# First input chunks loaded in three pieces of rows instead of one, two small copies issued from another queue, two matmuls moved later: a fused Fourier mixing and SoLU kernel

## The chip, the cores and the metric

The kernel runs on one core of one Trainium2 chip. The metric is device microseconds of one execution, the median over several runs. The profile is of one further execution, taken by the hardware profiler; its times are in microseconds (us) from the start of its span. PE is the matmul engine and PEld its weight load, DVE the vector engine, ACT the scalar engine, POOL GpSimd, SP the engine that here only issues DMAs; SPq and POOLq are the sequencers that issue them. L142 is line 142 of the kernel before; from L143 to the function `mean_out` the changed kernel's lines stand one higher.

## The reference

```python
# x (8, 3136, 256); w_in (256, 1024); w_out (1024, 256); g_ln (1024)
X = np.fft.fft(np.fft.fft(x, axis=1), axis=2).real      # over the sequence and over the features
t = X.reshape(25088, 256)
h = t @ w_in
sm = softmax(h)                                          # over the 1024 columns
solu = h * sm
ln = (solu - mean(solu)) / sqrt(var(solu) + 1e-6) * g_ln
out = ln @ w_out
```

All data are float32 in the device's memory, the weights in 64-bit pieces that the kernel narrows itself.

## The kernel before, in words

**The transform.** The 3136 positions are taken as 49 times 64, and the transform over the sequence is done in two matmul steps. Because only the real part is wanted, a row is always used together with its mirrored row, and the features are folded likewise before the product with `w_in`. The 8 batches go in 4 *pairs*; two batches of 49 rows are the 98 rows (`PR`) of a pair. A pair's 98 rows times 64 columns n2 are loaded in 8 *chunks* (`NC`) of 4 columns: `load` brings `xa`, the rows as they lie (L142, issued by SP, one DMA for a chunk), and `xb`, the mirrored rows (L144, an indirect DMA issued by POOL). For the first pair `rows` is 128 and not 98: 30 rows more are loaded than are used. A row of a chunk is 1024 floats, 4 KB. Chunks 0, 1, 6 and 7 lie in buffers of the pool `x`, chunks 2 to 5 in buffers named `room` that later hold `uT`.

For each chunk DVE adds the mirrored rows (`add_mirror`, L167 and L169) and folds the features (L174, L175, L182); PE makes `transform1` (L242); ACT copies the result `z` out of PSUM (L245). For the first pair this is the start of the program, and the next work on it follows from these chunks alone. SP keeps `z` in device memory (`zd`, L250), `turn` brings it back in another layout as `g` (L257, one half of the first part issued by SP and one by POOL), and `transform2` (L269) is made for each unit.

**The units.** After the start the program is a loop over 98 *units* of rows. For a unit: `transform2`, a copy to `q` (L275), a small copy `r` (`spread`, L280, SP), the product with `w_in` (`up`, L305), `even` (L318, DVE, output `ev`), `join` (L334 and L338, DVE, outputs `h` and its negated maximum `nmax`), the exponential (L346, ACT, reads `h` and `nmax`, output `u`), `product` (L353, DVE), `square` (L360, ACT), a transpose on DVE (L425, output `v`), 16 DMAs on SP for every second unit that move blocks of `v` to `uT` (L462), sums of blocks on POOL (L495, output `S`), seven block products in place of eight on PE (L502, `Ws` and `Wo` are made of `w_out`), with a copy on ACT between them (`seed`, L528), then the outputs `ot` and their stores (L600 on SP, L589 on POOL). PE's instructions of neighbouring units are interleaved.

**The half rows.** Two of the units, 90 and 91 in the order, come from rows that two batches share. One row of them (`q_half`) is computed for all batches at once by the class `Half`, in steps at units 86 to 89, and then `give` copies it into row 0 and every 32nd row of the unit's own `h` (4 rows of 4 KB) and `nmax` (4 values). These two copies are made once for each of the two units, on POOL's queue, after POOL's sums and before the run of 16 `uT` moves that SP issues at the even unit. ACT's second exponential of the unit reads them. (Such a unit runs its signs in the order 1, 0 at `join` and 0, 1 at the exponential.)

**The second weight at the start.** `raw_out`, the pieces of `w_out`, is loaded after the chunks; DVE narrows it in four steps to `Wo` (the last instruction of a step is L677). The mean of `w_out` over its rows is taken out of it: PE multiplies `ones` with the first four of the eight blocks of `Wo` (`mean_out(0)`, L782), and later with the sum of the other four, which POOL makes in `fold_out`; then `keep_mean` and `centre`.

**What sets the order.** The program is written inside `tc.manual_schedule()`: each engine runs its instructions in the order in which the code names them, and waits at each for the semaphores that the framework derives from the data. DMAs of SP count on eight semaphores in turn (`DMAHW0` to `DMAHW7` in the rows below), and each waits for the one issued eight places earlier to have landed.

Of the kernel before, what the change touches and what calls it, by code (L numbers as in the profile page):

```python
# [17 lines left out]
P = 128  # L18
# [5 lines left out]
NH = N2 // 2  # L24
PR = 2 * N1
# [30 lines left out]
def kernel(  # L56
# [76 lines left out]
    def load(pr, c, room=None):  # L133

        r = slice(pr.p * PR, (pr.p + 1) * PR)
        rows = PR if pr.p else P
        if room is None:
            xa = xpool.tile([P, CH, D], FP32, tag="xa", name="xa")
            xb = xpool.tile([P, CH, D], FP32, tag="xb", name="xb")
        else:  # L140
            xa, xb = (t.rearrange("p (l d) -> p l d", d=D) for t in room)
        nc.sync.dma_start(out=xa[0:rows], in_=x_pn[r.start : r.start + rows, c * CH + 1 : (c + 1) * CH + 1, :])  # L142
        i = pr.p * NC + c  # L143
        nc.gpsimd.indirect_dma_start(  # L144
            out=xb[0:rows].rearrange("p l d -> p (l d)"), out_offset=None, in_=x_g,
            in_offset=bass.IndirectOffsetOnAxis(ap=idx[0:rows, i : i + 1], axis=0))
        xa, xb = xa[0:PR], xb[0:PR]
        if c == NC - 1 and pr.p:
            load_zero(pr)
        pr.raw[c] = (xa, xb)  # L150
# [529 lines left out]
    class Weights:  # L680
# [91 lines left out]
            n = KF // 4 * D  # L772
            nc.gpsimd.tensor_tensor(out=self.part, in0=w[:, 0:n], in1=w[:, n:], op=ALU.add)

        def mean_out(self, half):
            if half == 0:
                self.cs = result(3)[:, 0:D]
                parts = [Wo[:, c, :] for c in range(KF // 2)]
            else:
                parts = [self.part[:, c * D : (c + 1) * D] for c in range(KF // 4)]  # L780
            for c, i in enumerate(parts):
                nc.tensor.matmul(self.cs, ones, i, start=half == 0 and c == 0, stop=half == 1 and c == KF // 4 - 1,  # L782
                                 skip_group_check=True)

        def keep_mean(self):
# [56 lines left out]
    class Half:  # L842
# [32 lines left out]

        def give(self, t):
            of = slice(4 * t.m, 4 * t.m + 4)
            nc.gpsimd.dma_start(out=t.h[1][0 : P : NH], in_=self.h[of])
            nc.gpsimd.dma_start(out=t.nmax[0 : P : NH, 1:2], in_=self.row[of, 1:2])

    with tc.manual_schedule():
        pairs = [Pair(p) for p in range(NP)]
# [124 lines left out]
        def begin(i):  # L1007

            cur = units[i]
            enter(i)  # L1010
            ps = up(cur, 0)
            if i in (2, 3):
                cur.odd = up(cur, 1)
                column(cur)
            even(cur, ps)
            if i not in (2, 3):
                cur.odd = up(cur, 1)
            second_transform(i + 2)
# [8 lines left out]
        for i in range(whole + 1):  # L1027
            cur = units[i]
            prv = units[i - 1] if i else None
            if prv:  # L1030
                turn_whole(prv, i == 1)
                if i == 1:
                    square(prv, 1)
            if i == 1:
                weights.mean_out(1)
            for s in cur.signs:
                join(cur, s)
            if i == 0:
                weights.narrow_out(3, (2,))
                weights.fold_out()  # L1040
            if 1 < i < whole:
                for o, ps in prv.wait:
                    nc.vector.tensor_copy(out=o, in_=ps)
            for s in cur.signs:
                expo(cur, s)
            if i == 1:
                weights.keep_mean()
            if i in (1, whole):
                for o, ps in prv.wait:
                    nc.scalar.copy(o, ps)  # L1050
            if i == 0:
                begin(1)
            done = units[0 if i == 2 else i - 1 : i] if i > 1 else []
            for t in done:
                stats(t)
            if i == whole:
                nxt = units[i + 1]
                enter(i + 1)
                even(nxt, up(nxt, 0))
            if i == whole:  # L1060
                other_pairs(i, ahead, "fold")
            for s in cur.signs:
                product(cur, s)
                if i < whole and s == 0:
                    square(cur, s)
            if i == 1:
                weights.centre(cur)
            if i == 2:
                weight_sums(cur)
            if i < whole:  # L1070

                if i:
                    begin(i + 1)
                if i:
                    square(cur, 1)
            else:
                for s in cur.signs:
                    square(cur, s)
                other_pairs(i, ahead, "mirror", cur)
                sums(units[1], None, part=slice(2, 4))  # L1080
                turn_both(cur)
                stats(cur)
            for work in ("mirror", "fold", "load") if i < whole else ("load",):
                other_pairs(i, ahead, work, cur)
            if i == whole - 1:
                sums(units[1], None, part=slice(0, 2))
            for t in done:
                power(t)
# [211 lines left out]
```

## Time and profile before

| | before |
|---|---|
| median of 3 runs (lowest to highest) | 1114.31 us (1113.95 to 1114.52) |
| the profiled execution's own time | 1113.99 us |
| its span, and PE's granted clock in it | 1112.2 us, 0.998 |
| PE busy | 1094.5 us, 98% |
| DVE busy | 971.2 us, 87% |
| ACT busy | 801.3 us, 72% |
| POOL busy | 786.6 us, 71% |
| DMA packets, bytes | 447594, 185.69 MB |

The time of the execution is 1.8 us over the span: what lies around the first and last instruction. An engine's share of the whole span says little of its share at the two places that the change touches, the first 90 us and the stretch of 1000 to 1025 us; those are read from windows of their own.

### The profile page before, as it was taken

The numbers are of one execution on the slowest core, as the hardware profiler recorded it, in microseconds if no ns is written. First come the engines' busy times: TensorE is split into PE (matmuls) and PEld (weight loads), VectorE is DVE, ScalarE is ACT, GpSimd is POOL, SyncE is SP. The second block draws the span as 40 slices with busy tenths as digits, with TensorE's granted clock in tenths as the row PEclk, the third lists the DMA queues.
The fourth block names the chain that finished last, engine by engine and source line by source line (L and its number), as shares of the span: only waits on it lengthen the run. The fifth ranks groups of instructions, "written<-read, shape, count | busy, mean of one in ns | idle before, by whom it ended". The sixth has DMA issues, their size and how long they took to land. (4 is left out here: it accounts for less than half of the span.)

```text
span 1112.2 us, 21997 instructions
## 1 busy us (share of the span) xinstructions
PE 1094.5 (98%) x7083; PEld 876.8 (79%) x7083; DVE 971.2 (87%) x1439; ACT 801.3 (72%) x1964; POOL 786.6 (71%) x661
## 2 busy tenths in 40 slices
PE   8899999999999999999999999999999999999998
PEld 5557878787887878788788787878878877777888
DVE  7998888889898898989989898888898898897984
ACT  5697777777777777777777777777777777676772
POOL 4066888775888878767778887856766766667665
PEclk9999999999999999999999999999999999999999
DMA  9654899878989989868989999976977878766775
GB/s 330 223 178 97 182 183 202 182 141 164 189 148 198 190 188 197 169 130 151 193 154 199 185 190 201 178 142 118 184 143 136 150 142 152 131 122 112 144 134 127
DMA packets 447594, 185.69 MB, mean 167 GB/s; under 512 B 415102, under 2 KB 429454, under 8 KB 447480
## 3 DMA queue, kind: packets, MB, share of 16 engines
q1 hardware_dynamic: 434760, 144.58, 68.5%
q0 software_dynamic: 12720, 39.69, 12.1%
q8 instruction: 58, 0.95, 0.3%
q14 instruction: 56, 0.46, 0.1%
HBM read 46.75 MB, written 38.80 MB: 77 GB/s over the span
## 5 line engine op out<-in xcount | busy, mean ns | idle before, releaser
L305 PE MATMUL ps_h<-Wi,q 128*128 128x512 f32 x768 | 346.7, 593 | 2.0 <-DVE nmax L338 1.7
L495 POOL TENSOR_TENSOR S<-uT 128x512 f32<-128x512 f32 x188 | 239.7, 1275 | 116.4 <-DVE u L353 50.6
L502 PE MATMUL ps_m<-Ws,S 128*128 128x128 f32 x2328 | 301.0, 275 | 2.5 <-POOL S L495 2.5
L502 PEld LDWEIGHTS ps_m<-Ws,S 128*128 128x128 f32 x2328 | 283.3, 192 | 7.8 <-POOL S L495 4.5
L360 ACT ACTIVATE h<-u,usum 128x1024 f32<-128x1024 f32 x196 | 225.0, 1148 | 68.6 <-DVE u L353 68.6
L305 PEld LDWEIGHTS ps_h<-Wi,q 128*128 128x128 f32 x768 | 138.4, 190 | 141.6 <-issue 136.6
L353 DVE SCALAR_TENSOR_TENSOR u<-h,u 128x1024 f32<-128x1024 f32 x196 | 233.7, 1228 | 15.9 <-ACT u L346 15.8
L346 ACT ACTIVATE u<-h,nmax 128x1024 f32<-128x1024 f32 x196 | 223.5, 1142 | 8.1 <-DMA nmax<-half 3.7
L425 DVE STREAM_TRANSPOSE v<-u 128x2048 f32<-128x2048 f32 x92 | 212.6, 2311 | 3.2
L502 PE MATMUL ps_m<-Wo,uT 128*128 128x128 f32 x1552 | 205.5, 275 | 0.0
L502 PEld LDWEIGHTS ps_m<-Wo,uT 128*128 128x128 f32 x1552 | 189.7, 192 | 2.0 <-issue 1.9
L338 DVE CUSTOM_DVE_ANT_0 h<-ev,ps_h 128x1024 f32<-128x1024 f32 x98 | 119.7, 1221 | 17.1 <-DVE ev L318 7.9
L338 DVE CUSTOM_DVE_ANT_0 h<-h,ps_h 128x1024 f32<-128x1024 f32 x96 | 117.2, 1221 | 14.0 <-ACT h L360 0.4
L589 POOL DMA_INDIRECT out_dram<-ot,idx x98 | 108.8, 1110 | 26.9 <-issue 11.5
L495 POOL TENSOR_TENSOR S<-S,uT 128x512 f32<-128x512 f32 x94 | 119.7, 1274 | 7.4
L495 POOL TENSOR_TENSOR S<-uT,S 128x512 f32<-128x512 f32 x94 | 119.8, 1275 | 7.3
L318 DVE SCALAR_TENSOR_TENSOR ev<-w_mid,r,ps_h 128x1024 f32<-128x1024 f32 x97 | 120.3, 1240 | 0.1
L502 PE MATMUL ps_m<-Ws,uT 128*128 128x128 f32 x776 | 102.7, 275 | 0.0
L502 PE MATMUL ps_m<-Wo,S 128*128 128x128 f32 x776 | 102.5, 275 | 0.0
L167 POOL TENSOR_TENSOR xa<-xa,xb 98x510 f32<-98x510 f32 (+1 forms) x48 | 59.3, 1236 | 56.8 <-DVE u L353 45.8
L537 ACT ACTIVATE ot<-ps_m,rs 128x256 f32<-128x256 f32 x97 | 45.9, 473 | 69.5 <-PE ps_m L502 50.3
L502 PEld LDWEIGHTS ps_m<-Ws,uT 128*128 128x128 f32 x776 | 94.7, 192 | 0.0
(141 smaller groups left out, 1191.7 us busy)
## 6 DMA issues: line engine op xcount, KB each, us to landing
uT<-v SPq DMA_DIRECT2D x736, 128.0 KB
out_dram<-ot SPq DMA_DIRECT2D x184, 64.0 KB
g<-zd POOLq DMA_DIRECT2D x18, 640.0 KB, 7.5
zd<-z SPq DMA_DIRECT2D x24, 400.0 KB
xa<-in_x_dram SPq DMA_DIRECT2D x24, 392.0 KB
raw_in<-in_moe_w_in_dram SPq DMA_DIRECT2D x4, 512.0 KB
xa<-in_x_dram SPq DMA_DIRECT2D x4, 512.0 KB
room<-in_x_dram SPq DMA_DIRECT2D x4, 512.0 KB
```

The lines of the kernel that those rows point to most:

```text
L167: i = engine.tensor_tensor(out=a[:, :, 1:D], in0=a[:, :, 1:D], in1=rb[:, :, D - 1 : 0 : -1], op=ALU.add)
L305: nc.tensor.matmul(ps[:, fs], t.q[:, c * P : (c + 1) * P], Wi[:, c, fs], start=True, stop=not whole_even)
L318: nc.vector.scalar_tensor_tensor(out=t.ev, in0=w_mid, scalar=t.r, in1=ps, op0=ALU.mult, op1=ALU.add)
L338: nc.vector.tensor_tensor_reduce(out=t.h[s], in0=t.h[0] if s else t.ev, in1=t.odd, scale=1.0 if s else -0.5, scalar=3.0e38, op0=ALU.add, o ...
L346: nc.scalar.activation(out=t.u[s], in_=t.h[s], func=ACT.Exp, bias=t.nmax[:, s : s + 1], scale=sign_of(t, s), accum_out=t.esum[:, s : s + 1])
L353: t.last = nc.vector.scalar_tensor_tensor(out=t.u[s], in0=t.h[s], scalar=sign_of(t, s), in1=t.u[s], op0=ALU.mult, op1=ALU.mult, accum_out= ...
L360: nc.scalar.activation(out=t.h[s], in_=t.u[s], func=ACT.Square, bias=t.usum[:, s : s + 1], scale=-float(FF), accum_out=t.ssq[:, s : s + 1])
L425: nc.vector.transpose(out=v, in_=u)
L495: i = engine.tensor_tensor(out=S[j], in0=a, in1=b, op=op)
L502: nc.tensor.matmul(o, a[:, c], b[:, c], start=start and c == 0, stop=c == n - 1, skip_group_check=True)
L537: nc.scalar.mul(out=self.t.ot[1], in_=self.PP, mul=self.rs[1])
L589: dma = nc.gpsimd.indirect_dma_start(out=out, out_offset=bass.IndirectOffsetOnAxis(ap=idx[:, i : i + 1], axis=0), in_=t.ot[s], in_offset=None)
```

## The change

It has three parts. (1) For the first pair, `xa` of a chunk is loaded in three DMAs, of rows 0 to 63, 64 to 95 and 96 to 97, instead of one of 128 rows. (2) The two copies of `give` are issued by SP instead of POOL. (3) `mean_out` is divided in three: the products of `ones` with blocks 0 and 1 of `Wo` stay where they were, those with blocks 2 and 3 come after `begin(1)` at unit 0, the last part stays.

```diff
 def load(pr, c, room=None):
...
-        nc.sync.dma_start(out=xa[0:rows], in_=x_pn[r.start : r.start + rows, c * CH + 1 : (c + 1) * CH + 1, :])
+        for a, b in ((0, PR),) if pr.p else ((0, 64), (64, 96), (96, PR)):
+            nc.sync.dma_start(out=xa[a:b], in_=x_pn[r.start + a : r.start + b, c * CH + 1 : (c + 1) * CH + 1, :])
...
-        def mean_out(self, half):
-            if half == 0:
+        def mean_out(self, part):
+            n = KF // 4
+            if part == 0:
                 self.cs = result(3)[:, 0:D]
-                parts = [Wo[:, c, :] for c in range(KF // 2)]
-            else:
-                parts = [self.part[:, c * D : (c + 1) * D] for c in range(KF // 4)]
-            for c, i in enumerate(parts):
-                nc.tensor.matmul(self.cs, ones, i, start=half == 0 and c == 0, stop=half == 1 and c == KF // 4 - 1,
+            for c in range(n):
+                i = self.part[:, c * D : (c + 1) * D] if part == 2 else Wo[:, part * n + c, :]
+                nc.tensor.matmul(self.cs, ones, i, start=part == 0 and c == 0, stop=part == 2 and c == n - 1,
                                  skip_group_check=True)
...
         def give(self, t):
             of = slice(4 * t.m, 4 * t.m + 4)
-            nc.gpsimd.dma_start(out=t.h[1][0 : P : NH], in_=self.h[of])
-            nc.gpsimd.dma_start(out=t.nmax[0 : P : NH, 1:2], in_=self.row[of, 1:2])
+            nc.sync.dma_start(out=t.h[1][0 : P : NH], in_=self.h[of])
+            nc.sync.dma_start(out=t.nmax[0 : P : NH, 1:2], in_=self.row[of, 1:2])
...
             if i == 1:
-                weights.mean_out(1)
+                weights.mean_out(2)
...
             if i == 0:
                 begin(1)
+                weights.mean_out(1)
```

What stands on SP's queue at the start, before. A row is a line, what it issues (output, input, shape), and the semaphores it waits for; `xa` and `room` are the chunks' buffers:

```order
L711 DMA gain<-in_moe_g_ln_dram 8x128
L142 DMA xa<-in_x_dram 128x1024 [waits DMAHW0_49]
L142 DMA xa<-in_x_dram 128x1024 [waits DMAHW1_49]
L142 DMA room<-in_x_dram 128x1024 [waits DMAHW2_49]
L142 DMA room<-in_x_dram 128x1024 [waits DMAHW3_49]
```

And with the change:

```order
L143 DMA xa<-in_x_dram 64x1024 [waits DMAHW0_49]
L143 DMA xa<-in_x_dram 32x1024 [waits DMAHW1_49]
L143 DMA xa<-in_x_dram 2x1024 [waits DMAHW2_49]
L143 DMA xa<-in_x_dram 64x1024 [waits DMAHW3_49]
L143 DMA xa<-in_x_dram 32x1024 [waits DMAHW4_49]
L143 DMA xa<-in_x_dram 2x1024 [waits DMAHW5_49]
L143 DMA room<-in_x_dram 64x1024 [waits DMAHW6_49]
```

Three issues stand for each one, 24 for 8 in all, and the eighth DMA ahead is two and two thirds chunks ahead instead of eight.

On SP's queue after the second of the two units with half rows, before: the stores of a unit before it, the small copy `r` of two units, and the next run of `uT` moves.

```order
L600 DMA out_dram<-ot_8896 32x2x256 [waits DMAHW5_49]
L600 DMA out_dram<-ot_8896 32x2x256 [waits DMAHW6_49]
L280 DMA r<-q 128x1x1 [waits DMAHW7_49,Activation_49]
L280 DMA r<-q 128x1x1 [waits DMAHW0_49,Activation_49]
L462 DMA uT<-v_8961 32x16x64 [waits DVE_49,DMAHW1_49,PE_49,Pool_49]
```

The same place with the change:

```order
L601 DMA out_dram<-ot_8912 32x2x256 [waits DMAHW7_49]
L601 DMA out_dram<-ot_8912 32x2x256 [waits DMAHW0_49]
L281 DMA r<-q 128x1x1 [waits DMAHW1_49,Activation_49]
L878 DMA h<-half 4x1024 [waits DMAHW2_49,DVE_49]
L879 DMA nmax<-half 4x1 [waits DMAHW3_49,DVE_49]
L281 DMA r<-q 128x1x1 [waits DMAHW4_49,Activation_49]
L463 DMA uT<-v_8977 32x16x64 [waits DVE_49,DMAHW5_49,PE_49,Pool_49]
```

The two copies stand behind the stores and the first `r`. On POOL's queue they stood, for that unit, between its sums and its store:

```order
L495 TENSOR_TENSOR S_106<-uT 128x512 [waits PE_49]
L878 DMA h<-half 4x1024 [waits DVE_49]
L879 DMA nmax<-half 4x1 [waits DVE_49]
L589 DMA out_dram<-ot_8976,idx 25088x256 [waits DMASW1_49]
L495 TENSOR_TENSOR S_105<-uT 128x512 [waits DMAHW4_49,DMAHW5_49,DMAHW3_49,DMAHW6_49,DVE_49,PE_49]
```

For the first of the two units they now stand on SP behind that unit's `r` and right ahead of the run of 16 `uT` moves.

On PE before, from the last product for the first weight on (`ps_m_104` takes the mean, `g` is the transformed half of the first pair):

```order
L731 MATMUL wps<-w_in,w_mid 128x512 x4
L782 MATMUL ps_m_104<-Wo,ones_ident 128x256 x4
L269 MATMUL ps_m_101<-T_88,g 128x128 x2
L269 MATMUL ps_m_102<-T_88,g 128x128 x2
L305 MATMUL ps_h_429<-Wi,q 128x512 x2
```

and with the change, the same place, up to the first transposes of unit 0, where the moved products now stand:

```order
L782 MATMUL ps_m_104<-Wo,ones_ident 128x256 x2
L270 MATMUL ps_m_101<-T_88,g 128x128 x2
L270 MATMUL ps_m_102<-T_88,g 128x128 x2
L306 MATMUL ps_h_443<-Wi,q 128x512 x2
L306 MATMUL ps_h_448<-Wi,q 128x512 x2
L270 MATMUL ps_m_101<-T_88,g 128x128 x2
L306 MATMUL ps_h_467<-Wi,q 128x512 x2
L306 MATMUL ps_h_472<-Wi,q 128x512 x2
L270 MATMUL ps_m_101<-T_88,g 128x128 x2
L782 MATMUL ps_m_104<-Wo,ones_ident 128x256 x2
L444 MATMUL ps_m_102<-ones_ident,u 128x128 x4
```

Two of the four products of the ones have left the place ahead of `transform2` of the first units.

## The prediction

> **What bounds the kernel now.** I read the page first. Its first two lines give PE's busy time and its share in 40 slices:
>
> ```profile
> PE 1094.5 (98%) x7083; PEld 876.8 (79%) x7083; DVE 971.2 (87%) x1439; ACT 801.3 (72%) x1964; POOL 786.6 (71%) x661
> PE   8899999999999999999999999999999999999998
> ```
>
> PE sets the time over most of the span, and is short of work at the start. Next come the stretches as windows; the columns are the window and its length, the busy time of PE, PEld, DVE, ACT and POOL, the granted clock, the DMA share and GB/s:
>
> ```profile
> 16.00:38.00 22.00, 19.68 (x81) 13.35 (x81) 18.98 (x38) 9.82 (x19) 2.84 (x3) 1.00 1.03 396
> 38.00:88.00 50.00, 45.67 (x191) 26.42 (x190) 47.33 (x85) 41.81 (x83) 22.53 (x21) 1.00 0.47 144
> 100.00:200.00 100.00, 100.00 (x656) 81.17 (x655) 89.71 (x138) 75.39 (x190) 82.50 (x66) 1.00 0.87 181
> 1000.00:1050.00 50.00, 47.52 (x310) 37.63 (x310) 42.36 (x62) 35.43 (x88) 33.94 (x31) 1.00 0.66 119
> ```
>
> From 100 us on PE has no idle time, except for 2.48 us of the window from 1000 us, where the copies of `give` are. So whatever the start loses, and whatever PE loses later, goes through to the end. In 16 to 38 us the DMA engines are full (share 1.03), and DVE then works nearly without a gap up to 88 us (47.33 of 50). So a delay of DVE at the chunks should also pass to the end. All three parts touch places where slack is small; 0.2% of the time, about what a measurement of this kernel can tell from no change, is 2.2 us.
>
> **Part 1, the chunks in pieces.** DVE's timeline has the three mirror adds of the first pair that wait for a load:
>
> ```profile
> 16.71 1.22 DVE L167 TENSOR_TENSOR xa<-xa,xb 98x1020 f32<-98x1020 f32 x1 [0.95 <-DMA xa<-in_x_dram]
> 24.39 1.22 DVE L167 TENSOR_TENSOR room<-room 98x1020 f32<-98x1020 f32 x1 [1.25 <-DMA room<-in_x_dram]
> 33.60 1.22 DVE L167 TENSOR_TENSOR xa<-xa,xb 98x1020 f32<-98x1020 f32 x1 [0.68 <-DMA xa<-in_x_dram]
> 36.20 0.68 DVE L167 TENSOR_TENSOR xa<-xa,xb 98x510 f32<-98x510 f32 x1
> ```
>
> They are chunks 0, 3 and 6; the last row is chunk 7's, with no wait. The DMA view of 16 to 24 us says how the two queues share:
>
> ```profile
> 16.00:24.00 8.00, 8.00 (x31) 5.18 (x31) 6.39 (x11) 2.88 (x7) 2.40 (x2) 1.00 1.03 409
> q0 software_dynamic: 449, 1.64, 51.5%
> q1 hardware_dynamic: 448, 1.63, 51.1%
> ```
>
> POOL's queue (`xb`, q0) and SP's (`xa`, q1) move the same, together 409 GB/s. A chunk is 128 rows of 4 KB twice, 1.05 MB, so a pair of loads takes 2.56 us; chunk 3's add at 24.39 less chunk 0's at 16.71 is 7.68, three times 2.56. The change takes 30 rows off `xa`: 401 KB and 524 KB, 2.26 us at the same rate. Counted in bytes alone a chunk would be 0.30 us shorter; but `xb` is not cut and gets half the engines, and it lands hardly before `xa` now:
>
> ```profile
> L144 POOL DMA_INDIRECT room<-in_x_dram,idx x2: 941/1014/1087, 11.2 to 12.6; - x2
> DMA to landing us min/median/max: 12.9/13.6/14.2
> ```
>
> The first of these two, chunk 3's, landed at 11.2 + 12.9 = 24.1, 0.3 us before its add. By bytes alone the gain is then that 0.3 or a little less, and chunk 6's wait of 0.68: together about 0.9 us.
>
> Against it stands what loads into fewer partitions moved. Two windows hold one alone, each on SP's queue: first the rest of the table `T`, issued at 54.20 into 64 partitions a DMA, then the second pair's `xa`, into 98:
>
> ```profile
> 54.20 1.22 SPq L716 DMA_DIRECT2D T<-in_t_tab_dram  x2
> ...
> 57.20:58.20 1.00, 0.24 (x2) 0.17 (x2) 1.00 (x3) 0.56 (x2) 1.00 (x1) 1.00 0.92 225
> 69.00:70.50 1.50, 1.20 (x4) 0.55 (x4) 1.50 (x5) 1.50 (x3) 0.86 (x1) 1.00 0.78 216
> ```
>
> With the engines 0.92 busy, 64 partitions took 225 GB/s, against 409 at 1.03 for 128. The new pieces are of 64 and 32 rows. No row shows a 32-row load from outside alone. Its ends are 112 GB/s, half of 225 by its partitions, and 409; I take 225, the row nearest in kind. Then a chunk is 96 rows of 4 KB, 393 KB at 225 GB/s = 1.75 us, and the last 2 rows with `xb`, 532 KB at 409 = 1.30 us: 3.05 instead of 2.56, 0.49 us more. Chunk 6 is the seventh pair to land, so its add starts 7 times 0.49 = 3.4 us later, and DVE's following work with it. (Chunk 7 lands 3.9 later, and had 1.1 us in hand before its add at 36.20, by the pace from chunk 6.) The ends: -0.9 us if bytes alone count; and if a piece slows all that is in flight with it, 925 KB at 225 / 0.92 = 245 GB/s is 3.78 us, 1.22 more, times seven +8.5 us. I take +3.4, since `xb` and the pieces are in flight together in every engine, and an engine that waits on a piece holds up the `xb` rows behind it only in part. The 16 more issues on SP lie ahead of the landings and cost nothing: one is 0.36 us by the row below, three a chunk are 1.1 of its 2.56 us or more, and the queue's depth of eight DMAs, two and two thirds chunks or 6.8 us, covers them. If that cover were short, the chunks would land later still.
>
> ```profile
> 22.89 0.36 SPq L142 DMA_DIRECT2D xa<-in_x_dram  x1
> ```
>
> The Trainium skill, in "SBUF — State Buffer", section "Door 1: The DMA port swizzle", says that partitions 0 to 63 reach 8 of 16 ports, and 0 to 31 the same 8, so that 32 rows move as fast as 64, at most 218 GB/s. The 225 beside it agrees for 64; by it the two pieces would take 393 KB / 218 = 1.80 us, and the part +3.8 us, where 112 GB/s for the 32 rows would give 1.17 + 1.17 us and +7.5.
>
> **Part 2, the copies of `give`.** Rows of SP, DVE, POOL, ACT and PE around the two units:
>
> ```profile
> 1001.29 13.35 SPq L462 DMA_DIRECT2D uT<-v  x16
> 1001.77 0.15 DVE L322 TENSOR_SCALAR nmax<-nmax 128x1 f32<-128x1 f32 x1
> 1002.80 0.59 POOL L879 DMA_DIRECT2D nmax<-half  x1
> 1006.71 1.15 ACT L346 ACTIVATE u<-h,nmax 128x1024 f32<-128x1024 f32 x1 [2.37 <-DMA nmax<-half]
> 1011.02 1.13 PE L502 MATMUL ps_m<-Ws,S 128*128 128x128 f32 x8 [1.46 <-POOL S L495]
> 1014.75 2.67 SPq L600 DMA_DIRECT2D out_dram<-ot  x4
> 1015.14 0.56 POOL L879 DMA_DIRECT2D nmax<-half  x1
> 1017.52 0.54 SPq L280 DMA_DIRECT2D r<-q  x1
> 1018.10 1.15 ACT L346 ACTIVATE u<-h,nmax 128x1024 f32<-128x1024 f32 x1 [1.37 <-DMA nmax<-half]
> 1022.41 1.13 PE L502 MATMUL ps_m<-Ws,S 128*128 128x128 f32 x8 [1.02 <-POOL S L495]
> ```
>
> ACT waits 2.37 and 1.37 us for the copies, and PE then 1.46 and 1.02 us. PE's releaser is named as POOL's sum, but ACT's copy `seed`, which stands behind the late exponentials on ACT, ends just before:
>
> ```profile
> 1010.65 0.27 ACT L528 COPY ps_m<-ps_m 128x128 f32<-128x128 f32 x1
> 1022.04 0.27 ACT L528 COPY ps_m<-ps_m 128x128 f32<-128x128 f32 x1
> ```
>
> The first copies, on SP, wait for DVE's `nmax` of 1001.77 only. Two issues of 0.6 us go ahead of the `uT` run. SP's small transfers at the start show the landing: `zd` is written at 41.33 and read back by the next issue at 43.27, so 1.94 us at most:
>
> ```profile
> 41.33 0.27 SPq L250 DMA_DIRECT2D zd<-z_g  x1
> 43.27 0.38 SPq L257 DMA_DIRECT2D g<-zd  x1
> ```
>
> They land at about 1001.9 + 1.2 + 1.4 = 1004.5 (POOL's landed just before 1006.71), and ACT's wait, which began at 1004.34, is gone, PE's 1.46 with it. But 0.6 us at the least and 1.2 at the most goes to the `uT` run behind them, on which everything on SP then stands. The second copies stand behind that run, the four stores and the first `r`: 1017.52 + 0.54 is 1018.06, and with 1.2 later 1019.3. Two issues of 0.6 and a landing of 0.9 to 1.9: 1021.4, for an exponential that now starts at 1018.10. So it is 3.3 us late (2.4 to 4.0) in the trace's own time; PE gets there 1.46 us earlier and then idles 1.02 + 3.3 + 1.46 = 5.8 us. As the time at which PE goes on is set by SP's queue, the first wait's gain is lost in it, and the part's sum is +3.3 us. The `uT` moves behind the copies are wanted by POOL's sums four units later, which covers 1.2 us. On POOL the two issues leave, 1.2 us a unit, where it is 34 of 50 us busy: no gain. The ends: -2.5 us if both of PE's waits go (1.46 and 1.02), +4.0.
>
> **Part 3, the products of the ones.** PE's rows, with DVE's and ACT's that decide:
>
> ```profile
> 46.19 1.13 PE L782 MATMUL ps_m<-Wo,ones_ident 128*128 128x256 f32 x4 [1.20 <-DVE Wo L677]
> 47.15 1.05 PE L269 MATMUL ps_m<-T,g 128*128 128x128 f32 x8
> 50.15 0.75 DVE L671 SCALAR_TENSOR_TENSOR S<-raw_out,top_bit,S 128x512 int32<-128x512 int32 x1
> 50.81 1.28 DVE L318 SCALAR_TENSOR_TENSOR ev<-w_mid,r,ps_h 128x1024 f32<-128x1024 f32 x1
> 58.03 2.13 PE L443 MATMUL ps_m<-ones_ident,u 128*128 128x128 f32 x13 [0.76 <-DVE u L353]
> 59.16 0.62 ACT L448 COPY uT<-ps_m 128x512 f32<-128x512 f32 x1
> ```
>
> PE waited 1.20 us for `Wo` and then took 1.0 us before `transform2`, which can now be up to 2 us earlier. But the next consumer on DVE, `ev`, begins at 50.81 straight behind DVE's own step of 50.15, with no idle time, so it gains nothing; at most about 1 us, were DVE ordered otherwise. The moved products fall in PE's idle 0.76 us ahead of 58.03 and overrun it by some 0.3, which ACT's copy at 59.16 may feel. I take 0, between -1.1 and +0.3.
>
> **The sum.** +3.4 + 3.3 + 0 = +6.7 us against the profiled execution, 1113.99 (1112.2 of span and 1.8 around it), which lies 0.3 under the median of 1114.31. On the median: 1121.0 us.
>
> **The rivals.** (a) Bytes alone count, and `give` is late: -0.9 + 3.3, 1116.7 us. For it speaks that `xb` fills the engines while a piece waits, so that the 409 GB/s may hold; against it that 225 was moved with engines 0.92 busy, not idle. The Trainium skill's page "DMA: Bandwidth & Descriptors" says in "Rules for kernel authors" that two transfers to disjoint halves share the same 16 engines and serialize, and advises one of 128 partitions; by it alone the pieces would be worth their bytes.
>
> (b) Faster: the copies on SP land in time. The place is ACT's exponential of unit 91: if SP gets to the second copies by 1016.5, that is if the `uT` run takes 3 us less than its 13.35 with no POOL issues beside it, both of PE's waits go, and with bytes alone the sum is -0.9 - 2.5: 1110.9 us. Against it: 0.83 us for each of 16 issues is the trace's own row.
>
> (c) The pieces slow the start and `give` gains: 3.4 - 2.5, 1115.2 us.
>
> (d) The pieces slow `xb` too: 8.5 + 3.3, 1126.1 us. For it: all engines serve both queues in turn.
>
> **How the numbers follow.** The two questions are nearly independent. I give contention of 3.4 with a late second copy 0.50, (a) 0.22, (b) 0.09, (c) 0.08, (d) 0.11. Faster by over 0.2% is (b), 0.09. Within 0.2%, 1112.1 to 1116.5, is (c) and somewhat under half of (a): 0.18. Slower is the rest, 0.73. The range leaves out (b) and the upper half of (d), 0.15, and takes in (c): 1115.0 to 1125.5. The likeliest case's own range is 1118.5 to 1123.5.
>
> **What would show it.** Part 1: the DMA rate in 16 to 24 us falls under 380 GB/s, and the mirror adds of chunks 3 and 6 come at about 25.9 and 37.0; a rate of 400 with chunk 3 by 24.3 shows (a). Part 2: ACT's wait for the first copy is gone, the second is issued by SP at about 1019 (plus the start's shift) and ACT and PE wait for it some 5 us. Part 3: `ev` starts no earlier against DVE's step before it. I would be wrong if the pieces, being packets of 4 KB as before, are limited only where they are alone, or if SP's `uT` run gets shorter.

## The result, and the profile after

| | before | with the change |
|---|---|---|
| median | 1114.13 us of 4 runs (1112.51 to 1114.52) | 1129.38 us of 4 runs (1127.50 to 1134.69) |
| ratio, 95% interval | | 1.0147 (1.0116 to 1.0177) |
| profiled execution: time, span, granted clock | 1113.99, 1112.2, 0.998 | 1127.50, 1125.6, 0.992 |

The change makes the kernel 15.3 us slower by the medians. The side was the forecast one; the size is over twice the 6.7 us that were forecast, and outside the range. The profiled execution is the fastest of the four and carries 13.4 us of it in its span; the traces can speak of those only.

Windows of the changed kernel, with the columns as in the prediction:

```profile
16.00:24.00 8.00, 7.27 (x25) 4.02 (x24) 5.04 (x9) 1.46 (x6) 2.25 (x3) 0.95 1.04 288
100.00:200.00 100.00, 100.00 (x644) 80.78 (x643) 86.16 (x131) 73.40 (x184) 79.95 (x65) 1.00 0.87 182
1000.00:1050.00 50.00, 43.45 (x283) 35.46 (x282) 38.55 (x58) 31.36 (x77) 27.30 (x23) 0.93 0.62 112
```

In 16 to 24 us the DMA engines are as full as before (1.04) and move 288 GB/s instead of 409. The steady part is as full as before. From 1000 us PE now lacks 6.6 us of 50, before it lacked 2.5, and the granted clock is 0.93 there.

The 13.4 us can be laid out in time with one instruction that every unit has, DVE's product. Its rows for unit 0, for a unit shortly before the half rows and for one behind them, with the change:

```profile
63.69 1.33 DVE L354 SCALAR_TENSOR_TENSOR u<-h,u 128x1024 f32<-128x1024 f32 x1
...
992.18 1.23 DVE L354 SCALAR_TENSOR_TENSOR u<-h,u 128x1024 f32<-128x1024 f32 x1 [0.16 <-ACT u L347]
...
1060.74 1.27 DVE L354 SCALAR_TENSOR_TENSOR u<-h,u 128x1024 f32<-128x1024 f32 x1 [0.30 <-ACT u L347]
```

The same instructions before:

```profile
56.63 1.33 DVE L353 SCALAR_TENSOR_TENSOR u<-h,u 128x1024 f32<-128x1024 f32 x1
...
984.00 1.23 DVE L353 SCALAR_TENSOR_TENSOR u<-h,u 128x1024 f32<-128x1024 f32 x1 [0.16 <-ACT u L346]
...
1047.31 1.28 DVE L353 SCALAR_TENSOR_TENSOR u<-h,u 128x1024 f32<-128x1024 f32 x1 [0.30 <-ACT u L346]
```

They come 7.06, 8.18 and 13.43 us later with the change. So 7.0 us are lost at the start, 5.25 at the half rows, and 1.2 in between, in two small steps (0.35 near unit 25, 0.8 near unit 50).

The start is seen in DVE's mirror adds of the changed kernel, chunks 0, 3 and 6:

```profile
18.84 1.22 DVE L168 TENSOR_TENSOR xa<-xa,xb 98x1020 f32<-98x1020 f32 x1 [2.58 <-DMA xb<-in_x_dram,idx]
28.79 1.22 DVE L168 TENSOR_TENSOR room<-room 98x1020 f32<-98x1020 f32 x1 [2.23 <-DMA room<-in_x_dram,idx]
40.19 1.22 DVE L168 TENSOR_TENSOR xa<-xa,xb 98x1020 f32<-98x1020 f32 x1 [1.71 <-DMA xa<-in_x_dram]
```

They stood at 16.71, 24.39 and 33.60: a chunk takes 3.32 us from 0 to 3 where it took 2.56. Chunk 0 is 2.1 us late already, chunk 6 is 6.6 us late. What DVE waits for at chunks 0 and 3 is now `xb`, the load that was not changed. POOL's queue (q0) in the DMA view of 16 to 24 us shows why:

```profile
q0 software_dynamic: 419, 1.54, 68.1%
q1 hardware_dynamic: 240, 0.76, 35.8%
```

The last number is the time that the packets took, as a share of 16 engines times 8 us: for q0 0.681 x 128 us / 419 = 208 ns a packet, and before 0.515 x 128 / 449 = 147 ns. These means have packets of 4 bytes in them, 42 and 48 of q0's. The trace's packets of 4 KB alone took 163 ns on both queues before; with the change they took 230 ns on `xb`'s queue and 243 ns on the pieces'. So the packets of `xb` take 1.4 times as long, with their rows and bytes unchanged, nearly as long as the pieces' own.

The half rows, rows of SP, ACT and PE:

```profile
1010.62 0.56 SPq L879 DMA_DIRECT2D nmax<-half  x1
1011.29 13.14 SPq L463 DMA_DIRECT2D uT<-v  x16
1024.54 2.36 SPq L601 DMA_DIRECT2D out_dram<-ot  x4
1027.00 0.55 SPq L281 DMA_DIRECT2D r<-q  x1
1028.37 0.54 SPq L879 DMA_DIRECT2D nmax<-half  x1
...
1012.42 1.13 ACT L347 ACTIVATE u<-h,nmax 128x1024 f32<-128x1024 f32 x1
1030.11 1.15 ACT L347 ACTIVATE u<-h,nmax 128x1024 f32<-128x1024 f32 x1 [7.67 <-DMA nmax<-half]
...
1034.41 2.05 PE L503 MATMUL ps_m<-Ws,S 128*128 128x128 f32 x8 [6.54 <-POOL S L496]
1036.25 1.61 PE L503 MATMUL ps_m<-Wo,uT 128*128 128x128 f32 x8
```

The first copies cost no wait any more (1012.42 has none; 2.37 us before). The second are issued behind 16 moves, four stores and an `r`, at 1028.37, and ACT waits 7.67 us, PE 6.54. Behind the idle time the first eight matmuls take 2.05 us, where they took 1.13.

### The profile page after: what moved, and what is told of

Read it like the earlier page. It is cut to its first block, busy times and chain, and to the rows that moved or that the text cites. A ratio compares the mean times of both kernels' runs of the same rounds, so it can differ in the third digit from the quotient of the medians.

```text
span 1125.6 us, 22023 instructions
## 1 busy us (share of the span) xinstructions
PE 1099.4 (98%) x7083; PEld 879.0 (78%) x7083; DVE 977.1 (87%) x1439; ACT 801.6 (71%) x1964; POOL 790.5 (70%) x657
## 4 chain that ended last, share of the span: by engine, by line
PE 87%; DMA 5%; SPq 3%; DVE 2%; POOL 1%; ACT 1%; issue 1%; POOLq 0%; DVEq 0%; ACTq 0%
PE ps_m L503 51%; PE ps_h L306 27%; PE ps_m L243 4%; PE ps_m L270 4%; SPq L463 2%; DMA xa<-in_x_dram 1%; POOL S L496 1%; DMA x<-in_x_dram 1%; DMA room<-in_x_dram 1%; DVE u L354 1%; PE ps_m L573 1%; DVE h L339 0%; DMA raw_in<-in_moe_w_in_dram 0%; DMA T<-in_t_tab_dram 0%; SPq L251 0%
## 5 line engine op out<-in xcount | busy, mean ns | idle before, releaser
L496 POOL TENSOR_TENSOR S<-uT 128x512 f32<-128x512 f32 x188 | 243.6, 1296 | 129.7 <-DVE u L354 59.4
L354 DVE SCALAR_TENSOR_TENSOR u<-h,u 128x1024 f32<-128x1024 f32 x196 | 238.7, 1253 | 20.1 <-ACT u L347 20.0
L270 PEld LDWEIGHTS ps_m<-T,g 128*128 128x128 f32 x400 | 59.7, 191 | 45.3 <-issue 43.1
L503 PEld LDWEIGHTS ps_m<-Wo,S 128*128 128x128 f32 x776 | 94.4, 192 | 0.0
```

The source lines that it names most:

```text
L270: nc.tensor.matmul(o, g[:, k, h * P : (h + 1) * P], table, start=(h == 0), stop=True, skip_group_check=True)
L354: t.last = nc.vector.scalar_tensor_tensor(out=t.u[s], in0=t.h[s], scalar=sign_of(t, s), in1=t.u[s], op0=ALU.mult, op1=ALU.mult, accum_out= ...
L496: i = engine.tensor_tensor(out=S[j], in0=a, in1=b, op=op)
L503: nc.tensor.matmul(o, a[:, c], b[:, c], start=start and c == 0, stop=c == n - 1, skip_group_check=True)
```

## The experiments

Each changes the kernel before, if nothing else is said. A run's own kernel before, on the same chip, had medians of 1112.5 to 1113.5 us.

### The parts one by one

**Part 1 alone** (`xa` of the first pair in pieces of 64, 32 and 2 rows, the first hunk of the diff).

> The kernel before with part 1 alone: the first pair's xa of a chunk in pieces of 64, 32 and 2 rows. If the start's shift in the changed kernel (DVE's products of unit 0 and of all later units 7.0 us later than before) comes from the pieces alone, the time is 1114.1 + 7.0 = 1121.1 us, the DMA rate in 16 to 24 us again about 288 GB/s instead of 409, and chunk 6's mirror add at about 40.2. By the prediction's own term it would be +3.4, 1117.5. If the start was lost through the moved products of the ones, there is no loss here.

1119.18 us, ratio 1.0063 (1.0047 to 1.0080): +7.0 by the ratio. The shift of the units in its trace is 6.7 us from unit 0 up to the half rows, with no step between. Behind them it is 5.2 us: there the first copies, still on POOL's queue, kept ACT waiting 0.49 us, against 2.37 before. In the eight traces of kernels that leave that place as it was, with both copies on POOL, this first wait lies between 0.49 and 2.37 us; the profile before has the longest. Its DMA window:

```profile
16.00:24.00 8.00, 6.31 (x18) 3.74 (x18) 5.68 (x10) 1.68 (x6) 2.21 (x2) 0.82 1.04 286
```

The pieces alone make the start's loss.

**Part 2 alone** (the copies of `give` on SP).

> The kernel before with part 2 alone: the two copies for each of the two units with half rows on SP. From the changed kernel's trace: the first wait of ACT gone (-2.5), the second 7.7 us long, together +5.3 us: 1119.4 us. The prediction's term was +3.3, 1117.4. If the fall of PE's granted clock in that stretch of the changed kernel (0.93 in 1000 to 1050 us) comes from PE's idle time there, it falls here too, and the matmuls behind the idle time are longer; if it belonged to the disturbed start, they are 1.13 us for 8 as before and the time is about 1118.

1119.46 us, ratio 1.0060 (1.0046 to 1.0075): +6.7 by the ratio. In its trace the units' shift goes from -0.8 at the start to +5.5, so 6.3 us are lost at the half rows, against the profile before with its first wait of 2.37 us. PE there:

```profile
1017.83 1.06 PE L502 MATMUL ps_m<-Ws,S 128*128 128x128 f32 x8
1025.59 2.04 PE L502 MATMUL ps_m<-Ws,S 128*128 128x128 f32 x8 [6.71 <-POOL S L495]
1027.43 1.91 PE L502 MATMUL ps_m<-Wo,uT 128*128 128x128 f32 x8
1029.14 1.68 PE L502 MATMUL ps_m<-Wo,S 128*128 128x128 f32 x8
1030.66 1.06 PE L502 MATMUL ps_m<-Ws,S 128*128 128x128 f32 x8
1031.55 3.60 PE L305 MATMUL ps_h<-Wi,q 128*128 128x512 f32 x8
```

and the granted clock in the second of these two windows is 0.57:

```profile
1020.00:1027.00 7.00, 1.41 (x6) 1.44 (x7) 4.41 (x4) 5.10 (x12) 2.90 (x3) 0.76 0.02 2
1027.00:1031.00 4.00, 4.00 (x23) 4.00 (x23) 2.83 (x6) 1.89 (x8) 2.40 (x3) 0.57 0.07 13
```

So the fall of the clock does not come from the start. It follows the idle time here too.

**Part 3 alone** (`mean_out` in three parts).

> The kernel before with part 3 alone: the products of the ones with blocks 2 and 3 of Wo later. The prediction's term: 0, between -1.1 and +0.3, so 1113.0 to 1114.4 us, with ev of unit 0 straight behind DVE's own step as before. If DVE's order leaves room, 1113.0.

1113.91 us, ratio 1.0005 (0.9994 to 1.0015): no change, as forecast. `transform2` of the first units begins at 45.63, 1.5 us earlier than before, and `ev` at 50.56 again straight behind DVE's own step of 49.90: the time that PE gains stops at DVE.

### What makes the loads slow

The forecast took the partitions that a piece reaches as the cause, and a moderate effect. The first run takes the bytes away without the pieces (the diffs here are shortened to the first pair's load).

```diff
-        nc.sync.dma_start(out=xa[0:rows], ...
+        nc.sync.dma_start(out=xa[0:98], ...      # rows112: 112, rows120: 120, of 128
```

> The kernel before with the first pair's xa loaded as one DMA of 98 rows for a chunk: the bytes of part 1 without its pieces. If the pieces are slow because of the partitions that they reach, 98 rows (64 below and 34 above row 64) are slow in part: 401 KB at the 216 GB/s of the second pair's load is 1.86 us and with xb 3.14, against 2.56 before: about +4 us at chunk 6, 1118. If the number of DMAs and their issues is what costs, there are as many as before and the bytes are fewer: -0.9, 1113.2 us.

1120.44 us, ratio 1.0061 (1.0046 to 1.0076). One DMA of 98 rows loses as much as three pieces do; neither the number of DMAs nor SP's issues are needed for the loss, and both theories' numbers were too small. Its trace has chunk 6 late by 6.2 us and unit 0 by 7.9.

```profile
16.00:24.00 8.00, 6.18 (x18) 3.56 (x18) 5.08 (x9) 1.63 (x6) 1.65 (x2) 0.83 1.01 277
```

The other 1.7 us are PE's. Its last 24 matmuls of `transform1`, before and here:

```profile
36.44 4.25 PE L242 MATMUL ps_m<-y,F 98*100 98x258 f32 x24 [1.83 <-DVE y L182]
...
42.60 7.04 PE L243 MATMUL ps_m<-y,F 98*100 98x258 f32 x24 [3.28 <-DVE y L183]
```

PE waits 3.28 us for the late chunk, and its granted clock from 43 to 48 us is 0.50, where it was 1.00 before. In the trace of part 1 alone the wait was 1.70 us, and the 24 took 4.25 us as before; in the changed kernel it was 2.85, and they took 5.80. So chunk 6 tells what the loads cost, and unit 0 may have a share of the clock in it.

Then all 128 rows in two DMAs, once as low and high half, once as even and odd rows:

```diff
+        for a, b in ((0, 64), (64, 128)):        # halves
+            nc.sync.dma_start(out=xa[a:b], in_=x_pn[r.start + a : r.start + b, ...])
+        for a in range(2):                       # even and odd
+            nc.sync.dma_start(out=xa[a : P : 2], in_=x_pn[r.start + a : r.start + P : 2, ...])
```

> The kernel before with the first pair's xa still of 128 rows, in two DMAs for a chunk: rows 0 to 63 and rows 64 to 127. Bytes as before, 1.05 MB for a chunk. If a load into 64 neighbouring partitions is slow by its partitions (225 GB/s alone), the rate in 16 to 24 us falls to 290 to 330 and the time rises by 5 to 8 us, to 1118 to 1121. If only the missing rows matter (98 of 128, whatever is done with them), or the share of the engines that a DMA reaches, the rate stays at 400 to 410 and the time at 1113.

> The kernel before with the first pair's xa of 128 rows in two DMAs of 64 rows for a chunk, the even rows and the odd rows: as many DMAs, rows and bytes as with two halves, but each DMA reaches partitions all over the 128. If what counts is which partitions are reached, the rate is that of before, 400 to 410 GB/s, and the time 1113 within 1.5 us. If it is the number of rows in a DMA or the number of DMAs, it is as slow as with two halves.

The halves: 1124.26 us, ratio 1.0105 (1.0089 to 1.0120). Even and odd: 1112.99 us, ratio 0.9997 (0.9988 to 1.0006). The windows and the two queues, the halves first:

```profile
16.00:24.00 8.00, 6.54 (x24) 3.77 (x23) 4.34 (x7) 1.66 (x5) 1.34 (x2) 1.00 1.04 283
q0 software_dynamic: 326, 1.20, 54.2%
q1 hardware_dynamic: 325, 1.07, 49.3%
```

and the even and odd rows:

```profile
16.00:24.00 8.00, 6.66 (x29) 4.50 (x28) 6.67 (x11) 2.67 (x5) 2.40 (x2) 1.00 1.03 410
q0 software_dynamic: 469, 1.72, 54.0%
q1 hardware_dynamic: 472, 1.55, 48.8%
```

As many DMAs, rows and bytes, and 283 against 410 GB/s. A packet of `xb`'s queue takes 0.542 x 128 / 326 = 213 ns beside the halves, and 147 ns beside even and odd rows, as before. Which rows a DMA holds decides, and it sets the time of the other queue's packets too.

Is it the reach, then, the partitions that a DMA leaves out? With 112 and with 120 rows every stretch of the 128 but the last is reached:

> The kernel before with the first pair's xa as one DMA of 112 rows for a chunk (14 useless rows instead of 30). The even and odd halves cost nothing and the low and high halves 11 us, so which rows stand in a DMA decides; but 98 rows in one DMA lost 7.8 us, more than the 4 that its partitions give. Two theories: by reach (a DMA is slow in so far as its rows leave partitions out) 112 rows are nearly as good as 128, 409 GB/s, and the time 1112.5 to 1114. By alignment (128 rows over 16 engines are 8 each, and each engine keeps to its own group of partitions; with 112 it is 7 each and two engines meet in a group) the packets of xa and xb get longer, the rate in 16 to 24 us falls to 280 to 340, and the time rises by 4 to 8 us, 1117 to 1121.

> The same with 120 rows. By reach: as before, 1112.5 to 1113.5. By alignment it depends on how the rows are dealt out: 15 engines with 8 rows each keep to their own groups and the time is 1112.5 to 1113.5; 16 engines with 7 or 8 each do not, and it is 1116 to 1121.

1121.41 us, ratio 1.0074 (1.0058 to 1.0091), and 1123.78 us, ratio 1.0092 (1.0079 to 1.0105). The windows of 112 rows and of 120 rows:

```profile
16.00:24.00 8.00, 7.10 (x25) 3.78 (x23) 4.72 (x8) 1.97 (x7) 1.70 (x2) 1.00 1.04 261
```

```profile
16.00:24.00 8.00, 7.05 (x25) 3.78 (x23) 4.83 (x9) 2.04 (x6) 1.72 (x2) 1.00 1.03 287
```

The reach theory falls: leaving out 8 rows costs more than leaving out 30. The loads know two rates here. DMAs of all 128 rows, or of every second row of them, run at 410 GB/s with `xb` beside them; 98, 112 or 120 rows, two halves and the pieces run at 261 to 288, and among these more bytes mean more time at chunk 6:

| `xa` of a chunk | KB with `xb` | GB/s, 16 to 24 us | chunk 6 later by, us | unit 0 later by, us |
|---|---|---|---|---|
| 128 rows, one DMA (before) | 1049 | 409 | 0 | 0 |
| even and odd rows | 1049 | 410 | -0.2 | -0.2 |
| 98 rows | 925 | 277 | 6.2 | 7.9 |
| 64 + 32 + 2 rows | 925 | 286 | 6.7 | 6.8 |
| 112 rows | 983 | 261 | 7.0 | 8.8 |
| 120 rows | 1016 | 287 | 8.2 | 9.4 |
| 64 + 64 rows | 1049 | 283 | 8.6 | 9.4 |

One rule that could part the two rates is that the rows must be dealt to the engines so that no two write into the same group of partitions at a time. It fits 120 rows only if they are not dealt as 15 engines of 8 rows each, the case in which their expectation had no loss. How rows are dealt out is in no view of the profile, so the rule stays a guess, and why these loads have two rates stays open. The Trainium skill describes the deal for 128 rows in "DMA: Bandwidth & Descriptors", section "The descriptor swizzle": each engine then writes to one port only. No run shows the ports; the full rate of the 128 rows, 409 GB/s, agrees with it. The Trainium skill, on the same page under "Back-pressure in remote DMA", says that a full port holds up the other queues of the engine that waits for it; it says so of copies between cores. The 147 and 213 ns of `xb` would fit the like for loads of one core, but no run shows a stalled write.

### The half rows

> The kernel before with the copies of the first unit with half rows on SP and those of the second on POOL. In the changed kernel the first ones gained 2.5 us before the second ones lost. If the second unit's copies on POOL stay where they were in relation to PE, the gain stays: 1110.2 us. If they are tied to POOL's own sums, whose blocks come from SP's run of uT, which starts 1.2 us later behind the copies, the gain is lost at the second unit: 1112.7 to 1114.

```diff
+            (nc.gpsimd if t.m % 2 else nc.sync).dma_start(...)     # both copies
```

1112.23 us, ratio 0.9995 (0.9986 to 1.0004). In the trace the units behind the half rows gain 2.2 us against those ahead of them, so the second copies did stay with PE; but the runs do not show a gain of 2.2 us. Part of the 2.2 may belong to the profile before: with both copies on POOL, the traces of 98, 112 and 120 rows, of the halves and of the even and odd rows also gain 0.7 to 1.2 us there. So this one is not settled.

> The kernel before with the two copies of each unit with half rows issued by ACT, which is the engine that waits for them, in the idle time ahead of its exponentials (0.57 and 2.05 us). Two issues of about 0.6 us on ACT, no queue ahead. If the landing is as quick as on SP (the first copies there: under 2 us), both waits go: -2.5 us, 1110.3; if ACT's issues delay its first exponential by what they take, -2.5 + 0.6 for the first unit and 0 for the second: 1110.8; if ACT's queue is as slow as POOL's (3 to 4 us to land), 1112 to 1113.

```diff
-            nc.gpsimd.dma_start(...)
+            nc.scalar.dma_start(...)                               # both copies
```

1116.96 us, ratio 1.0035 (1.0021 to 1.0049): slower, which none of the three branches of the expectation had. Waits of SP in this run:

```profile
SPq L462 <- DMA h<-half: 13.5, 1, 13.5
SPq L462 <- DMA nmax<-half: 0.5, 1, 0.5
```

The copies issued by ACT take their turn in the eight semaphores that SP's DMAs count on. In the middle of its run of 16 moves for the units before, SP came to the one that a copy was to free, and waited 13.5 us for that copy's data to be made and landed; the move itself reads nothing of the copy. ACT's own wait was gone for the first copies and 1.18 us for the second (1.37 on POOL); another queue paid.

> Part 2 alone on SP, but of the run of 16 uT moves that stands ahead of the second unit's copies only 8 are left there; the other 8 are issued behind the copies. If the second copies are late because of their place in SP's queue, they now start as soon as DVE's nmax is there, land under 2 us later, and both of ACT's waits go: about 2.5 to 3.3 us faster than before, 1110 to 1110.6, and PE has no idle time of over 1 us there. If they are late for another reason (the copies themselves, or DVE's nmax), the loss of about 6 us stays: 1119.

```diff
-                move_blocks(batches[i // 2 - 1], slice(0, 2))
+                move_blocks(batches[i // 2 - 1], slice(0, 2), rows=range(2 if i == SELF_AT else 4))
+            if i == SELF_AT + 1:                   # behind the second give
+                move_blocks(batches[i // 2 - 1], slice(0, 2), rows=range(2, 4))
```

(with `give` on SP.) 1110.95 us, ratio 0.9979 (0.9970 to 0.9989): faster than both kernels, by 0.2% against the one before. SP's queue there:

```profile
1003.66 6.46 SPq L462 DMA_DIRECT2D uT<-v  x8
1010.24 2.38 SPq L600 DMA_DIRECT2D out_dram<-ot  x4
1012.71 0.55 SPq L280 DMA_DIRECT2D r<-q  x1
1013.36 0.59 SPq L878 DMA_DIRECT2D h<-half  x1
1014.05 0.54 SPq L879 DMA_DIRECT2D nmax<-half  x1
1014.63 6.13 SPq L462 DMA_DIRECT2D uT<-v  x8
```

The second copies go out at 1014.05, and ACT still waits 1.1 us for them. PE's window, 49.99 us of work in 50:

```profile
1000.00:1050.00 50.00, 49.99 (x334) 40.26 (x334) 44.98 (x63) 38.05 (x95) 33.20 (x29) 1.00 0.72 127
```

With eight moves fewer ahead of the copies the whole loss is gone, so the place in SP's queue was its cause.

To weigh the clock apart, PE was given matmuls to do in the idle time of part 2 alone; they are written over before use:

```diff
+                if i == SELF_AT + 2:
+                    for _ in range(40):              # then 20, and 26
+                        nc.tensor.matmul(new.X, ident, Wo[:, 0, 0:P], start=True, stop=True, ...)
```

> Part 2 alone on SP, with 40 matmuls of 128 columns more on PE, written over before use, in the time in which PE waits for the second copies (about 5 us of its 6.7 us). They compute nothing that is needed. If the granted clock falls because PE stands idle, and the fall to 0.57 costs the 2.3 us by which the next four products (5.96 us from the first's start to the next up, 3.64 before) are longer, then the clock stays near 1 here and the time is 2.3 us less than with part 2 alone, 1117.2 against 1119.5. If the clock has another cause, the products are as long as there and the time is the same.

1120.86 us, ratio 1.0067 (1.0054 to 1.0080). The 40 took 9.1 us, longer than the idle time, so PE was late by its own filler, and the time proves nothing. But the products behind them were 1.06 us each, and the clock 1.00.

> As with the 40 matmuls more, but 20 of them (4.5 us by the 9.1 us that the 40 took, of the 6.7 us in which PE stood idle), so that they end before the second copies' exponential lets PE go on. If the fall of the clock after the idle time costs 2.3 us, the four products are 1.06 us each as with the 40, and the time is about 2.3 us less than with part 2 alone on SP: 1117.2 where that was 1119.5. If the idle time left after them (about 2 us) is enough to lower the clock, or the fall has another cause, the time is 1119.5.

1119.57 us, ratio 1.0058 (1.0044 to 1.0072), the same as part 2 alone by the runs. In the trace the half rows lose 3.9 us instead of 6.3, but its start and its middle are 2.8 us later than in the profiled execution of part 2 alone.

> Part 2 alone on SP with 26 matmuls more (about 6.0 us of the 6.7 us in which PE stood idle), beside part 2 alone on the same chip. With 20 the trace had the stretch 2.4 us shorter (shift of the later units over it 3.9 us, 6.3 without), and the four products at 1.06 us each, but the medians of two different calls differ by 0.1 us only, with the start of the profiled executions 2.8 us apart. If the clock's fall costs 2.3 us, this run is 1.5 to 2.5 us faster than part 2 alone beside it. If the filler gives no time back, they are the same.

> Part 2 alone on SP, to stand beside the run with 26 matmuls more on the same chip: again about 6.5 us over the kernel before, with PE idle for 6.7 us and four products of 2.04, 1.91, 1.68 and 1.06 us after it.

Side by side on one chip: 1118.02 us (1117.12 to 1118.92) with the 26 matmuls, 1119.61 us (1119.38 to 1119.79) without; ratios to before 1.0046 (1.0032 to 1.0060) and 1.0059 (1.0045 to 1.0074). The five runs of each do not overlap. PE with the 26:

```profile
1026.34 1.13 PE L502 MATMUL ps_m<-Ws,S 128*128 128x128 f32 x8 [0.88 <-ACT ps_m L528]
1027.31 1.06 PE L502 MATMUL ps_m<-Wo,uT 128*128 128x128 f32 x8
1028.20 1.06 PE L502 MATMUL ps_m<-Wo,S 128*128 128x128 f32 x8
1029.09 1.06 PE L502 MATMUL ps_m<-Ws,S 128*128 128x128 f32 x8
1029.98 3.60 PE L305 MATMUL ps_h<-Wi,q 128*128 128x512 f32 x8
```

From the first product to the next `up` it is 3.64 us here, 5.96 us in part 2 alone (1025.59 to 1031.55) and 6.59 us in its repeat. The repeat had PE idle for 6.66 us, as expected, but its four products took 2.05, 1.92, 1.91 and 1.50 us: the clock was 0.50 through the whole of 1027 to 1031. More work on PE makes the kernel faster: the clock's fall behind 6.7 us of idle time costs 2.3 and 2.9 us in the two traces, and 1.6 us between the medians. The releaser of the first product is named here as ACT's `seed`, as the prediction had read it.

### The change, mended

> The changed kernel with the first pair's xa again as one DMA of 128 rows, part 2 with 8 of the 16 uT moves behind the second unit's copies, and part 3 as changed. If the three parts' costs are as told (the pieces all of the start's loss, the queue place all of the second copies' loss, the moved products nothing), the time is that of the half run alone, 1111, 0.2% under the kernel before. If part 3 costs or gains something beside them, it differs from 1111 by that.

1112.41 us, ratio 0.9991 (0.9982 to 1.0000): no more than the kernel before, and not shown to be faster than it; 1111 was expected. With the two causes taken away, no loss is left. Its profiled execution gains 2.4 us at the half rows and is 1.2 us late at the start and 0.8 more near unit 25. The start is again PE's clock: chunk 6 came 0.9 us earlier than before, but from 36 to 42 us the clock was 0.50, and the last 24 matmuls of `transform1` took 7.48 us instead of 4.25. PE's wait ahead of them was only 1.72 us, no longer than the 1.83 before, so what let the clock fall in this execution is not shown.

## Why the prediction was wrong in size and right in its places

**The start, +3.4 forecast, +7.0 measured (6.7 in the trace of part 1 alone).** The failed step is "I take +3.4, since ... an engine that waits on a piece holds up the `xb` rows behind it only in part". It holds them up nearly as long as the piece itself: `xb`'s packets of 4 KB took 230 ns instead of 163, the pieces' 243. So the 1.30 us for the last 2 rows with `xb`, at the full 409 GB/s, is the term that was too small; all that is in flight went at 288 GB/s. From chunk 0 to chunk 3 a chunk took 3.32 us, not 3.05, which over the six steps to chunk 6 makes 1.6 us. The other 1.6 us stand in chunk 0, 2.1 us late where one pair was counted, 0.49: the loads of the next chunks are in flight with it, and in 8 to 16 us the rate was already 268 GB/s, against 342 before. Together chunk 6 was 6.6 us late.

The prediction's upper end (3.78 us a chunk, +8.5 us) had the mechanism, with too low a rate. Rival (d), with its chance of 0.11, had it too, and its 8.5 us was nearer to 7.0 than 3.4 was. The 225 GB/s of the load into 64 partitions, taken as the price of the piece alone, was the sign to read for both queues: with the engines at 0.92 the load filled their time, not only its own share. The signs named for it came out beyond the forecast in the same direction: the rate under 380 (288), chunk 3 at 25.9 (28.79), chunk 6 at 37.0 (40.19). (By four pairs of 0.49 us the forecast for chunk 3 would have been 26.4.)

The partitions reached, the other half of that step's reason, are not the whole cause: one DMA of 120 rows is as slow. The rule that the prediction weighed from the Trainium skill, "SBUF — State Buffer", section "Door 1: The DMA port swizzle", goes by the ports that are reached; by it the even and odd rows are fast and the halves slow, as measured, but 112 and 120 rows should be nearly full, and the runs decide against that. (The 225 GB/s of 64 partitions lie 3% over the 218 that it gives as the most.) And rival (a), with the rule that pieces are worth their bytes, fell with the halves.

**The half rows, +3.3 forecast, +5.25 in the changed kernel, 6.3 in part 2 alone.** The queue's working held: the first wait gone, the run of `uT` 1.2 us later, the second copies behind it and the stores. In part 2 alone ACT's exponential stands at 1021.29, 1022.1 without the 0.8 us that its execution started earlier; forecast was 1021.4. So late landing made 4.0 of the 6.3, the top of the stated 2.4 to 4.0; the terms as listed give 2.7 to 4.3, and 1021.4 goes by the shortest landing. The failed step here is a term put at nothing, the clock: 2.3 us in part 2 alone, and in the changed kernel 5.08 us from 1034.41 to the next `up` at 1039.49 instead of 3.64, 1.4 us. The prediction foresaw 5.8 us without work on PE and priced it as idle time only. The Trainium skill has the rule, in "TensorE: Matmul & The Clock Gate", section "Why this matters for your kernels": over about 3 us without work put PE back to half its clock. The trace agrees, with a granted clock of 0.57 and eight matmuls in 2.04 us instead of 1.13 after 6.7 us. The length of the wait alone does not tell it in this case: the clock also fell in the mended kernel's start, where PE's last wait was 1.72 us.

**Part 3, 0 forecast, +0.6 (-0.7 to +1.7) measured.** Right, and for the reason given.

**The rest.** The middle's 1.2 us were not forecast. There DVE's product and POOL's sum are twice as long, at the same time:

```profile
310.80 2.29 POOL L496 TENSOR_TENSOR S<-uT 128x512 f32<-128x512 f32 x1
...
311.88 2.29 DVE L354 SCALAR_TENSOR_TENSOR u<-h,u 128x1024 f32<-128x1024 f32 x1
```

Steps of together 0.3 to 1.4 us are also in the middle of the traces of 98 and 120 rows, of the halves, of the even and odd rows, of the first copies on SP alone, of the 20, 26 and 40 matmuls and of the mended kernel. None is in those of the three parts alone, of 112 rows, of the copies on ACT and of the divided run. They go with no part of the change; what starts them is open. So is the rest of the 15.3 us: 13.4 are in the trace, and the other three runs of the changed kernel were slower than the one with the trace. The parts alone add up to 7.0 + 6.7 + 0.6 = 14.3 us, within the interval of the whole (12.9 to 19.7).

## What to carry to other kernels

When a transfer is cut or divided, price what it does to everything that shares its engines, not the transfer alone: 30 useless rows in a DMA of 128 were cheaper than any way tried of leaving them out. Before a small copy is moved to another queue, list what stands ahead of it there at its time, and what the queue's semaphores will wait for; where no place is free, divide the run in front of it. An idle time of several us on PE can cost more than its length, so add the slow matmuls behind it to the price.

## What the runs showed of the hardware that was not expected

- Loads of 120 of 128 rows, with a full load on the other queue, ran at 287 GB/s, both queues together, against 409 for all 128; pairs of loads of 64 rows in steps of two ran at the full rate (410), of 64 neighbouring rows at 283.
- A load that is slow lengthens the packets of the other queue's load, from 147 to 213 ns in the mean of the queue.
- After 6.7 us without work, which ended at 1025.59, PE's granted clock was 0.57 over 1027 to 1031 (0.50 in the repeat). 26 useless matmuls in that time made the kernel 1.6 us faster.
- A DMA that ACT issues takes its turn in the semaphores that SP's DMAs count on: SP waited 13.5 us for it.
